# Decays of a gated linear-attention kernel taken from sums of logarithms, with a written order on every engine

## The chip, the cores and the metric

The kernel runs on one core of a Trainium2 chip. The metric is device time in microseconds (us), as the median of several executions. The before kernel's runs are 1266.61 to 1267.79 us, median 1267.73 us (3 runs). Engines are named as in the profile: PE is TensorE (matmuls), PEld its weight loads, DVE is VectorE, ACT is ScalarE, POOL is GpSimd, SP issues the DMAs.

## The reference, cut to what matters

Two blocks follow each other. The first is a recurrence over 768 time steps for each of 4 batches and 8 heads, with 48 channels a head; the second is an MLP on the 3072 tokens, with an activation h * erf(softplus(h)).

```python
f = 1.0 / (1.0 + np.exp(-f_logit))                  # (4, 8, 768, 48)
for t in range(S):
    state = f[:, :, t, :, None] * state + einsum('bhd,bhe->bhde', k[:, :, t], v[:, :, t])
    y[:, :, t] = einsum('bhd,bhde->bhe', q[:, :, t], state)
x = y.transpose(0, 2, 1, 3).reshape(3072, 384)      # heads side by side
h = x @ w_in                                        # w_in 384 x 2048, float64 in memory
sp = np.maximum(h, 0) + np.log1p(np.exp(-np.abs(h)))
out = (h * erf(sp)) @ w_out                         # w_out 2048 x 384, float64 in memory
```

The logits are drawn with mean 2 and deviation 0.5, q, k and v with mean 0 and deviation 0.1.

## The kernel before, in words

Time is cut into 24 chunks of 128 steps (6 a batch) and 8 blocks of three chunks (384 tokens). For a chunk, f, q and k are loaded with time on the partitions and turned by TensorE so that channels lie on the partitions (two heads at a time, at partitions 0 and 64). Within a chunk, output t needs the score of every earlier step s, weighted for each channel with the product of the decays between s and t. The kernel makes these without a division or a logarithm, by doubling. `scores` (line 332) computes the scores of all 8 heads and `keep` (lines 343 and 351) writes only those whose s and t first part at the current level; then `Q` is multiplied by one half's decay products on DVE (line 365), `K` by the other half's on POOL (line 369), and the products themselves are doubled on POOL (line 374). That is one set of scores at the start and one for each of seven levels, 8 sets a chunk, and set n+1 waits for the multiplications after set n. The decays come from Exp, an addition and a reciprocal (lines 313 to 315). Then `y` is summed from the kept scores `At` times v and from `Q` times the state (lines 383 and 387), copied, turned back by TensorE (`ps_x`, line 423) and copied into `xT`; the state is renewed through `ps_k`, `dS` and `S_new`.

The MLP of a block (`second_part`) has 48 matmuls into `hps` (line 255), copied by ACT to `Hg` (line 263), an activation on four groups of 128 x 1536 numbers (Exp, Ln, four Squares on ACT, four products on DVE, Tanh on ACT, one more product on DVE; lines 235 to 245), and 48 matmuls into `ops` (line 269), copied (line 278) and stored. It is a generator: `chunk` calls `pump` behind each set of scores, which issues some of the last block's matmuls there. On each engine the order is that in which a scheduler placed the program's instructions; tile pools with two buffers decide when a tile is free. The float64 weights are rounded to float32 on DVE with seven operations for each of 16 pieces of 128 x 768 (`round_piece`, lines 160 to 177); no MLP matmul stands ahead of the third chunk's end.

## Time and profile before

| what | value |
|---|---|
| median of 3 runs | 1267.73 us (1266.61 to 1267.79) |
| the profiled execution | 1266.82 us; its span 1264.8 us |
| PE busy, mean granted clock | 1045.9 us (83%), 0.889 of full speed |
| PEld, DVE, ACT, POOL busy | 693.3, 767.9, 574.3, 330.7 us |
| DMA | 37.18 MB, mean 29 GB/s |

A busy share says how long an engine had an instruction in work, not that it ran at its peak. The granted clock is 1.0 at 2.4 GHz and 0.5 at 1.2 GHz; a stretch between the two held both. A float32 matmul of the program leaves two records in the trace, a transpose one.

### The profile page before, as it was taken

To read this page: it belongs to the slowest core of one execution; us is meant where nothing else is said; L and a number is where in the kernel's file an instruction comes from. 1 tells how busy PE (TensorE), PEld (TensorE's weight loads), DVE (VectorE), ACT (ScalarE), POOL (GpSimd) and SP (SyncE) were. 2 spreads that over 40 slices of the span, in tenths; PEclk is the share of its full clock that TensorE was granted. 3 is DMA by queue.
4 is the path that set the end of the run, shared out by engine and by line. 5 is a ranking of instruction groups with operands and counts; after the bars stand their busy time and mean duration, and the time that the engine had idled before them with its cause. 6 is when DMAs were issued, how large, how long until landed. Compare 5 with 4: busy or idle time off the path is not lost.

```text
span 1264.8 us, 15677 instructions
## 1 busy us (share of the span) xinstructions
PE 1045.9 (83%) x6456; PEld 693.3 (55%) x6456; DVE 767.9 (61%) x752; ACT 574.3 (45%) x629; POOL 330.7 (26%) x369
## 2 busy tenths in 40 slices
PE   3252678898988899898978899898979899889877
PEld 2141565565655566565656566565656566556444
DVE  7979426666476816765476825864576735972262
ACT  0010114762286515771277316761387217751692
POOL 2726212213232303213232313322231312321000
PEclk9999859888888889888888889888888889888888
DMA  9530100101110110110110110110111000000000
GB/s 250 155 94 25 25 14 13 25 12 28 32 25 2 25 32 13 25 25 13 32 25 8 25 39 1 26 26 20 25 26 25 13 8 1 1 1 20 0 1 19
DMA packets 108742, 37.18 MB, mean 29 GB/s; under 512 B 100480, under 2 KB 103552, under 8 KB 108672
## 3 DMA queue, kind: packets, MB, share of 16 engines
q1 hardware_dynamic: 108672, 36.18, 13.2%
q8 instruction: 51, 0.84, 0.3%
q14 instruction: 19, 0.16, 0.0%
HBM read 31.46 MB, written 4.72 MB: 29 GB/s over the span
## 4 chain that ended last, share of the span: by engine, by line
PE 48%; DVE 21%; ACT 13%; POOL 12%; issue 5%; SPq 1%; DMA 0%; POOLq 0%; DVEq 0%; ACTq 0%
PE ops L269 15%; PE sc L332 10%; POOL K L369 8%; PE hps L255 7%; PE y L383 6%; PE y L387 5%; DVE e L241 5%; DVE F L315 5%; POOL T L374 4%; ACT x L238 3%; DVE Hg L245 2%; DVE At L343 2%; ACT z L236 2%; ACT e L235 2%; ACT L236 2%
## 5 line engine op out<-in xcount | busy, mean ns | idle before, releaser
L332 PE MATMUL sc<-Q,K 48*128 48x128 f32 (+2 forms) x3456 | 226.4, 280 | 169.7 <-POOL K L369 90.1
L332 PEld LDWEIGHTS sc<-Q,K 48*128 48x128 f32 (+2 forms) x3456 | 190.2, 184 | 271.1 <-POOL K L369 146.9
L255 PE MATMUL hps<-xT,w_in_sb 128*128 128x384 f32 x768 | 309.8, 540 | 12.0 <-ACT Hg L263 11.3
L269 PE MATMUL ops<-w_out_sb,Hg 128*128 128x384 f32 x768 | 301.9, 541 | 14.1 <-DVE Hg L245 8.8
L369 POOL TENSOR_TENSOR K<-K,T 128x256 f32<-128x256 f32 x144 | 191.9, 1333 | 354.3 <-PE sc L332 354.3
L241 DVE SCALAR_TENSOR_TENSOR e<-x,e 128x1536 f32<-128x1536 f32 x128 | 228.6, 1792 | 81.7 <-ACT x L238 81.2
L238 ACT ACTIVATE x<-z,serf_bias 128x1536 f32<-128x1536 f32 x128 | 200.4, 1572 | 83.7 <-DVE e L241 83.6
L269 PEld LDWEIGHTS ops<-w_out_sb,Hg 128*128 128x128 f32 x768 | 153.0, 210 | 114.6 <-issue 24.5
L255 PEld LDWEIGHTS hps<-xT,w_in_sb 128*128 128x128 f32 x768 | 148.2, 209 | 100.7 <-issue 19.5
L343 DVE COPY_PREDICATED At<-masks,sc 128x1024 f32<-128x1024 uint8 x144 | 186.7, 1297 | 0.1
L365 DVE TENSOR_TENSOR Q<-Q,T 128x256 f32<-128x256 f32 x144 | 80.1, 556 | 148.8 <-PE sc L332 148.7
L374 POOL TENSOR_TENSOR T<-F 128x256 f32<-128x256 f32 x24 | 34.3, 1429 | 459.0 <-DVE F L315 459.0
L351 ACT COPY At<-sc 32x256 f32<-32x256 f32 (+1 forms) x72 | 31.2, 433 | 178.1 <-PE sc L332 177.7
L263 ACT COPY Hg<-hps 128x384 f32<-128x384 f32 x128 | 58.7, 471 | 110.1 <-PE hps L255 110.0
L383 PE MATMUL y<-vt,At 128*128 128x48 f32 x384 | 84.1, 318 | 0.0
L315 DVE RECIPROCAL F<-F 128x512 f32<-128x512 f32 x24 | 80.5, 3353 | 0.8
L387 PE MATMUL y<-S_new,Q 48*128 48x48 f32 x320 | 79.8, 335 | 1.0 <-DVE Q L365 1.0
L374 POOL TENSOR_TENSOR T<-T 128x128 f32<-128x128 f32 (+1 forms) x144 | 72.1, 501 | 11.3
L383 PEld LDWEIGHTS y<-vt,At 128*128 128x128 f32 x384 | 66.2, 220 | 13.8 <-ACT At L351 0.4
L416 DVE TENSOR_TENSOR S_new<-S_new,dS 128x192 f32<-128x192 f32 x16 | 5.7, 355 | 106.4 <-PE dS L406 106.4
L278 ACT COPY osb<-ops 128x384 f32<-128x384 f32 x24 | 11.5, 479 | 127.2 <-PE ops L269 127.2
L387 PEld LDWEIGHTS y<-S_new,Q 48*128 48x128 f32 x320 | 57.8, 225 | 11.7 <-DVE Q L365 1.4
(61 smaller groups left out, 747.8 us busy)
## 6 DMA issues: line engine op xcount, KB each, us to landing
raw<-in_moe_w_in_dram SPq DMA_DIRECT2D x8, 768.0 KB, 7.5
raw<-in_moe_w_out_dram SPq DMA_DIRECT2D x8, 768.0 KB, 4.2
f_nat<-in_f_logit_dram SPq DMA_DIRECT2D x24, 192.0 KB, 3.2
q_nat<-in_q_dram SPq DMA_DIRECT2D x24, 192.0 KB, 3.9
k_nat<-in_k_dram SPq DMA_DIRECT2D x24, 192.0 KB, 3.7
vt<-in_v_dram SPq DMA_DIRECT2D x24, 192.0 KB, 2.7
out_dram<-osb SPq DMA_DIRECT2D x24, 192.0 KB, 1.9
```

Of the source, the lines that this page charges most:

```text
L238: nc.scalar.activation(out=x[:], in_=z[:], func=AF.Square, bias=serf_bias[:, i : i + 1], scale=SERF_K)
L241: nc.vector.scalar_tensor_tensor(out=e[:], in0=x[:], scalar=b, in1=e[:], op0=ALU.add, op1=ALU.mult)
L255: nc.tensor.matmul(hps[:, 0:TB], lhsT=w_in_sb[:, kt, ft * P : (ft + 1) * P], rhs=xT[:, kt, :], start=(kt == 0), stop=(kt == n_k - 1),)
L269: nc.tensor.matmul(ops[:, 0:d_model], lhsT=groups[ft // FG][:, ft % FG, tt * P : (tt + 1) * P], rhs=w_out_sb[:, ft, :], start=(ft == 0), s ...
L315: nc.vector.reciprocal(out=F[:], in_=F[:])
L332: nc.tensor.matmul(sc[s0 : s0 + size, r, a, s0 + off : s0 + off + size], lhsT=K[rows(r), a, s0 : s0 + size], rhs=Q[rows(r), a, s0 + off : ...
L343: nc.vector.copy_predicated(out=A[:].rearrange("s r a t -> s (r a) t"), mask=masks[:, level, :].unsqueeze(1).broadcast_to((P, H, P)), data ...
L365: nc.vector.tensor_tensor(out=Qv[:, :, 1, :], in0=Qv[:, :, 1, :], in1=Tv[:, :, 0:1].broadcast_to((P, n, h)), op=ALU.mult,)
L369: nc.gpsimd.tensor_tensor(out=Kv[:, :, 0, :], in0=Kv[:, :, 0, :], in1=Tv[:, :, 1:2].broadcast_to((P, n, h)), op=ALU.mult,)
L374: nc.gpsimd.tensor_tensor(out=T2[:], in0=Tv[:, :, 0], in1=Tv[:, :, 1], op=ALU.mult)
L383: nc.tensor.matmul(y_h, lhsT=A[:, r, a, :], rhs=vt[:, 2 * a + r, :], start=True, stop=(c == 0))
L387: nc.tensor.matmul(y_h, lhsT=Q[rows(r), a, :], rhs=S_old[rows(r), a, :], start=False, stop=True)
```

## The change

The decays are no longer multiplied up by levels. With c the running sum over the chunk of log(1 + exp(-logit)), q is multiplied by exp(-c) and k by exp(c), and one set of scores under a triangular mask replaces the eight. `prepare` makes the logarithms with a maximum on POOL and Exp and Ln on ACT, one call for a block's three chunks; `stage_d` sums them with one matmul by a triangular matrix, takes the two exponentials from PSUM and multiplies q on DVE and k on POOL; four DMAs bring the chunk's last row of exp(-c), which is the chunk's whole decay, onto partitions as `Tall`. `stage_t` turns q and k, `stage_s` makes the scores, masks them on DVE (`A`) and forms the new state `Mbd`. `stage_y` makes x already transposed: v and the state are the stationary operand, 32 columns each, and A or q moves, so that each matmul writes 32 partitions of `y`; no transposes or second copy follow. The rows of `w_in` are loaded in the order that this leaves.

Rounding now has an Abs on ACT, a maximum on POOL, four operations on DVE and the last addition on POOL. Hidden rows are copied from PSUM by DVE, two tiles of 384 at a time. The whole order is written by hand: `slots` yields 96 MLP matmuls for a block (the hidden matmuls of block `it` and the output matmuls of block `it - 1`), every third slot takes one step of the activation, and the 12 stages of block `it + 1` are spread over the slots. The first and the last iteration have 48 slots, and the last two have no stages. At the end the smallest whole decay is compared with `GUARD`, and where it is smaller, `general()` computes everything again by levels.

```diff
+GUARD = 4.3e-18
+LOGIT_MIN = -43.0
...
-        sc, blocks = scores(0)
-        pump(fill)
-        nc.vector.tensor_tensor(out=Q[:], in0=Q[:], in1=F[:], op=ALU.mult)
-        keep(sc, blocks, 0)
...
-        for level, h in enumerate(levels):
-            sc, blocks = scores(h)
-            pump(fill)
...
-            nc.vector.tensor_tensor(
-                out=Qv[:, :, 1, :], in0=Qv[:, :, 1, :],
-                in1=Tv[:, :, 0:1].broadcast_to((P, n, h)), op=ALU.mult,
-            )
-            nc.gpsimd.tensor_tensor(
-                out=Kv[:, :, 0, :], in0=Kv[:, :, 0, :],
-                in1=Tv[:, :, 1:2].broadcast_to((P, n, h)), op=ALU.mult,
-            )
-            T2 = work.tile([P, n], FP32, name=f"T{h}", tag=f"T{h}")
-            nc.gpsimd.tensor_tensor(out=T2[:], in0=Tv[:, :, 0], in1=Tv[:, :, 1], op=ALU.mult)
-            T = T2[:]
...
+    def y_matmuls(y, A, vt, qT, Mbd):
...
+        for i in range(2):
+            for h in range(4 * i, 4 * i + 4):
+                nc.tensor.matmul(
+                    y[M * (h % 4) : M * (h % 4 + 1), i, :],
+                    lhsT=v_heads(vt, h % 2)[:, h // 2, mains(h % 2)],
+                    rhs=A[:, h % 2, h // 2, :],
+                    start=True, stop=last, skip_group_check=True,
+                )
...
+        nc.scalar.activation(out=x.bitcast(FP32), in_=high.bitcast(FP32), func=AF.Abs)
+        nc.gpsimd.tensor_scalar(
+            out=x.bitcast(FP32), in0=x.bitcast(FP32), scalar1=TINY, scalar2=None, op0=ALU.max
+        )
         nc.vector.tensor_scalar(
+            out=x, in0=x, scalar1=0x07FFFFFF, scalar2=3,
+            op0=ALU.bitwise_and, op1=ALU.logical_shift_left,
+        )
+        nc.vector.scalar_tensor_tensor(
+            out=x, in0=high, scalar=0xC0000000, in1=x, op0=ALU.bitwise_and, op1=ALU.bitwise_or
         )
         nc.vector.tensor_scalar(
+            out=z, in0=x, scalar1=0xFF800000, scalar2=None, op0=ALU.bitwise_and
+        )
+        nc.vector.scalar_tensor_tensor(
+            out=low.bitcast(FP32), in0=low, scalar=2.0**-52, in1=z.bitcast(FP32),
+            op0=ALU.mult, op1=ALU.mult,
+        )
+        nc.gpsimd.tensor_tensor(
+            out=dst,
+            in0=low.bitcast(FP32).rearrange("p (a f) -> p a f", a=dst.shape[1]),
+            in1=x.bitcast(FP32).rearrange("p (a f) -> p a f", a=dst.shape[1]),
+            op=ALU.add,
...
+    def prepare(blk, j0, j1):
+        lt = lts[blk][:, j0:j1, :].rearrange("t j c -> t (j c)")
+        nc.gpsimd.tensor_scalar(
+            out=lt, in0=lt, scalar1=LOGIT_MIN, scalar2=None, op0=ALU.max
+        )
+        nc.scalar.activation(out=lt, in_=lt, func=AF.Exp, scale=-1.0)
+    def prepare_log(blk, j0, j1):
+        lt = lts[blk][:, j0:j1, :].rearrange("t j c -> t (j c)")
+        nc.scalar.activation(out=lt, in_=lt, func=AF.Ln, bias=1.0)
+    def stage_d(g):
+        blk, j = divmod(g, CPB)
+        ps = ps_at.tile([P, 512], FP32, name="ps_d", tag="at")
+        nc.tensor.matmul(
+            ps[:, 0:d_model], lhsT=tri[:], rhs=lts[blk][:, j, :], start=True, stop=True
+        )
+        dp = dps[g % 2]
+        dm = work1.tile([P, d_model], FP32, name="dm", tag="dm")
+        nc.scalar.activation(
+            out=dp[:, :, 0:D], in_=ps[:, 0:d_model].rearrange("t (h d) -> t h d", d=D),
+            func=AF.Exp, scale=-1.0,
+        )
+        nc.scalar.activation(out=dm[:], in_=ps[:, 0:d_model], func=AF.Exp)
+        for a in range(HP):
+            nc.sync.dma_start(
+                out=Tall[:, g, a : a + 1], in_=dp[P - 1 : P, 2 * a : 2 * a + 2, :]
+            )
+        for eng, dst, n, d in (
+            (nc.vector, qds[g % 2], qns[g % NQ], dp[:, :, 0:D]),
+            (nc.gpsimd, kds[g % 2], kns[g % NQ], dm[:].rearrange("t (h d) -> t h d", d=D)),
+        ):
+            eng.tensor_tensor(
+                out=dst[:, :, 0:D],
+                in0=n[:].rearrange("t (h d) -> t h d", d=D),
+                in1=d,
+                op=ALU.mult,
+            )
+    def stage_t(g):
+        pss = []
+        for src in (qds[g % 2], kds[g % 2]):
+            ps = ps_at.tile([P, HP, P], FP32, name="ps_t", tag="at")
+            flat = src[:].rearrange("t (a r) d -> t a (r d)", r=2)
+            for a in range(HP):
+                nc.tensor.transpose(ps[:, a, :], flat[:, a, :], ident[:])
+            pss.append(ps)
+        qTs[g] = work.tile([P, HP, P], FP32, name="qT", tag="qT")
+        kTs[g] = work1.tile([P, HP, P], FP32, name="kT", tag="kT")
+        nc.scalar.copy(out=qTs[g][:], in_=pss[0][:])
+        nc.vector.tensor_copy(out=kTs[g][:], in_=pss[1][:])
+    def stage_s(g):
+        b, c = divmod(g, NCH)
+        qT, kT = qTs[g], kTs.pop(g)
+        sc = ps_sc.tile([P, 2, HP, P], FP32, name="sc", tag="sc")
+        for a in range(HP):
+            for r in range(2):
+                nc.tensor.matmul(
+                    sc[:, r, a, :], lhsT=kT[rows(r), a, :], rhs=qT[rows(r), a, :],
+                    start=True, stop=True,
+                )
+        A = work1.tile([P, 2, HP, P], FP32, name="A", tag="A")
+        nc.vector.tensor_tensor(
+            out=A[:].rearrange("s r a t -> s (r a) t"),
+            in0=sc[:].rearrange("s r a t -> s (r a) t"),
+            in1=mask[:].unsqueeze(1).broadcast_to((P, H, P)),
+            op=ALU.mult,
+        )
+        As[g] = A
+        if c == NCH - 1:
+            return
+        dS = ps_at.tile([P, HP, D], FP32, name="dS", tag="at")
+        vt, kd = vts[g % NV], kds[g % 2]
+        for a in range(HP):
+            for r in range(2):
+                h = 2 * a + r
+                nc.tensor.matmul(
+                    dS[rows(r), a, :], lhsT=kd[:, h, 0:D], rhs=v_heads(vt, r)[:, a, :],
+                    start=True, stop=True,
+                )
...
+            nc.vector.tensor_tensor(
+                out=Sn[rows(r)], in0=dS[rows(r)], in1=old[rows(r), :, r, :], op=ALU.add
+            )
+            nc.gpsimd.tensor_tensor(
+                out=new[rows(r), :, r, :], in0=Sn[rows(r)], in1=total, op=ALU.mult
+            )
+    def stage_y(g):
+        c = g % NCH
+        blk, j = divmod(g, CPB)
+        if j == 0:
+            xTs[blk] = work.tile([P, n_k, TB], FP32, name="xT", tag="xT")
+        y = ps_at.tile([P, n_k, P], FP32, name="y", tag="at")
+        y_matmuls(y, As.pop(g), vts[g % NV], qTs.pop(g), Mbds[(g + 1) % 2] if c else None)
+        nc.scalar.copy(out=xTs[blk][:, :, j * P : (j + 1) * P], in_=y[:])
...
+        y = work1.tile([P, FG * TB], FP32, name="yl", tag="yl")
+        nc.scalar.activation(out=y[:], in_=e[:], func=AF.Ln, scale=SERF_C, bias=1.0)
+        yield
+        x = None
+        for i in range(len(SERF_AB)):
+            x_new = work.tile([P, FG * TB], FP32, name="x", tag="x")
+            squared(x_new, y, i)
+            if x is not None:
+                times(e, x, i - 1)
+            x = x_new
+            yield
+        times(e, x, len(SERF_AB) - 1)
+        yield
+        yield
         nc.scalar.activation(out=e[:], in_=e[:], func=AF.Tanh)
+        yield
         nc.vector.tensor_tensor(out=h, in0=h, in1=e[:], op=ALU.mult)
...
+                    while not gr["done"]:
+                        act_step()
...
+        if it < last:
+            return chain(
+                *(hidden(it, gi) for gi in range(n_g - 1)),
+                *(project(it - 1, [tt], whole) for tt in range(CPB)),
+                hidden(it, n_g - 1),
+            )
+        if it == last:
...
+            return chain(
+                *(hidden(it, gi) for gi in range(n_g - 1)),
+                *(project(it - 1, [tt], whole) for tt in range(CPB - 1)),
+                some(FG),
+                hidden(it, n_g - 1),
+                head,
+            )
+        return project(last, list(range(CPB)), [range(n_ft - FG), range(n_ft - FG, n_ft)])
...
+        prepare(0, 0, 1)
+        prepare_log(0, 0, 1)
+        stage_d(0)
+        prepare(0, 1, 3)
+        prepare_log(0, 1, 3)
+        stage_t(0)
+        stage_d(1)
+        stage_s(0)
+        weights_step()
+        stage_t(1)
+        stage_y(0)
+        stage_d(2)
+        stage_s(1)
+        weights_step()
+        stage_t(2)
+        stage_y(1)
+        stage_s(2)
+        load_to(3)
+        weights_step()
+        stage_y(2)
...
+            for g in range(g0, g0 + CPB):
+                last = g == n_chunks - 1
+                todo += [] if last else [(stage_d, g + 1)]
+                todo += [(stage_s, g)]
+                todo += [] if last else [(stage_t, g + 1)]
+                todo += [(stage_y, g)]
...
+            for s, _ in enumerate(slots(it)):
+                if it == 0 and s % 6 == 2:
+                    weights_step()
+                if it == 0 and s % 6 == 5:
+                    weights_step()
...
+                if at and s == at[0]:
+                    at.pop(0)
+                    f, g = todo.popleft()
+                    f(g)
+                    if f is stage_y:
+                        load_to(g + LOOK)
+                if s % 3 == 2:
+                    act_step()
+                if it + 2 < n_blocks and s == n // 2:
+                    prepare(it + 2, 0, CPB)
+                    prepare_log(it + 2, 0, CPB)
...
+        low = work.tile([P, 1], FP32, name="low", tag="low")
+        nc.vector.tensor_reduce(
+            out=low[:], in_=Tall[:].rearrange("p g a -> p (g a)"), axis=AX.X, op=ALU.min
...
+    bad = nc.values_load(flag[0:1, 0:1], min_val=0, max_val=1)
+    with tc.If(bad > 0):
+        general()
```

The places below show how the instructions stand on their engines. On PE, within a steady block of the kernel before (`sc` are sets of scores, `hps` hidden matmuls, `ops` output matmuls):

```order
L332 MATMUL sc<-Q,K 128x128 x8
L255 MATMUL hps<-xT,w_in_sb 128x384 x7
L332 MATMUL sc<-Q,K 128x128 x8
L255 MATMUL hps<-xT,w_in_sb 128x384 x2
L332 MATMUL sc<-Q,K 128x128 x8
L255 MATMUL hps<-xT,w_in_sb 128x384
L332 MATMUL sc<-Q,K 128x128 x8
L255 MATMUL hps<-xT,w_in_sb 128x384 x3
L332 MATMUL sc<-Q,K 128x128 x8
L255 MATMUL hps<-xT,w_in_sb 128x384 x5
```

Five of the eight sets of one chunk stand here between the MLP matmuls.

On PE, within a steady block now (`ps_d` is the sum of logs, `ps_t` the transposes; Hg with a number is one group's buffer):

```order
L450 MATMUL hps<-xT,w_in_sb 128x384 x7
L312 MATMUL ps_d<-lt,tri 128x384
L450 MATMUL hps<-xT,w_in_sb 128x384 x5
L476 MATMUL ops<-w_out_sb,Hg_113 128x384 x2
L356 MATMUL sc<-qT,kT 128x128 x8
L375 MATMUL dS<-vt_92,kd_102 48x48 x8
L476 MATMUL ops<-w_out_sb,Hg_113 128x384 x2
L476 MATMUL ops<-w_out_sb,Hg_114 128x384 x4
L476 MATMUL ops<-w_out_sb,Hg_115 128x384 x2
L343 MATMUL ps_t<-ident,qd_101 128x128 x4
L343 MATMUL ps_t<-ident,kd_103 128x128 x4
L476 MATMUL ops<-w_out_sb,Hg_115 128x384 x2
```

One chunk's sum, one set of scores with its `dS`, and the transposes stand about seven MLP matmuls apart.

On DVE before, while weights are rounded (`raw`, `w_x`, `w_z`, `w_e` belong to the rounding, the rest to the first chunk):

```order
L170 SCALAR_TENSOR_TENSOR w_e<-raw,w_z 128x768
L160 TENSOR_SCALAR w_x<-raw 128x768
L173 TENSOR_TENSOR w_e<-w_e,w_x 128x768
L174 TENSOR_SCALAR w_z<-raw 128x768
L164 SCALAR_TENSOR_TENSOR w_x<-raw,w_x 128x768
L177 SCALAR_TENSOR_TENSOR w_in_sb<-w_z,w_e 128x3x256
L167 TENSOR_SCALAR w_z<-w_x 128x768
L343 COPY_PREDICATED At_91<-masks,sc 128x1024
```

And now on DVE in the first MLP iteration (`w_t` and Hg_112 upward are the rounding's buffers):

```order
L273 TENSOR_SCALAR w_t<-w_t 128x768
L277 SCALAR_TENSOR_TENSOR w_t<-Hg_112,w_t 128x768
L280 TENSOR_SCALAR w_t<-w_t 128x768
L283 SCALAR_TENSOR_TENSOR Hg_112<-Hg_112,w_t 128x768
L330 TENSOR_TENSOR qd_100<-qn_95,dp_104 128x8x48
L273 TENSOR_SCALAR w_t<-w_t 128x768
L277 SCALAR_TENSOR_TENSOR w_t<-Hg_113,w_t 128x768
L280 TENSOR_SCALAR w_t<-w_t 128x768
L283 SCALAR_TENSOR_TENSOR Hg_113<-Hg_113,w_t 128x768
```

with this on POOL at the same place:

```order
L270 TENSOR_SCALAR w_t<-w_t 128x768
L287 TENSOR_TENSOR w_in_sb<-Hg_112,w_t 128x3x256
L300 TENSOR_SCALAR lt<-lt 128x768
L330 TENSOR_TENSOR kd_102<-kn_98,dm 128x8x48
L270 TENSOR_SCALAR w_t<-w_t 128x768
L287 TENSOR_TENSOR w_in_sb<-Hg_113,w_t 128x3x256
L391 TENSOR_TENSOR Mbd_107<-Sn,Tall 48x4x48 x2
L270 TENSOR_SCALAR w_t<-w_t 128x768
```

Each piece stands between a maximum and an addition on POOL, in one line with the chunks' work of that engine, and DVE's first of four operations waits for the maximum.

On ACT in a steady block now (half a block; `yl` is the activation's logarithm, `lt` the logits):

```order
L411 ACTIVATE e<-Hg_113 128x1536
L413 ACT_TABLE_LOAD
L413 ACTIVATE yl<-e 128x1536
L170 ACTIVATE x<-yl,serf_bias 128x1536 x2
L317 ACT_TABLE_LOAD
L317 ACTIVATE dp_104<-ps_d 128x8x48
L321 ACTIVATE dm<-ps_d 128x384
L170 ACTIVATE x<-yl,serf_bias 128x1536 x2
L426 ACTIVATE e<-e 128x1536
L347 COPY qT<-ps_t 128x512
L411 ACTIVATE e<-Hg_114 128x1536
L413 ACT_TABLE_LOAD
```

A block has 10 table loads: four ahead of the activation's Ln, three ahead of `stage_d`, two in `prepare`, one ahead of a Tanh.

## Rows read from the trace of the kernel before

**Rows 1.** Busy time by stretch (us): opening, two steady blocks, tail; then clock, DMA share, GB/s.

```profile
0.00:183.00 183.00, 80.15 (x597) 67.05 (x597) 132.94 (x195) 12.36 (x23) 72.16 (x61) 0.91 0.39 95
566.50:846.50 280.00, 252.99 (x1620) 166.17 (x1618) 172.43 (x154) 143.31 (x158) 75.36 (x88) 0.89 0.11 22
1160.00:1264.80 104.80, 84.37 (x237) 48.13 (x235) 35.17 (x21) 60.86 (x57) 0.01 (x1) 0.86 0.02 8
```

**Rows 2.** Groups of instructions by shape: busy us, mean ns; idle before, releasers.

```profile
L269 PE MATMUL ops<-w_out_sb,Hg 128*128 128x384 f32 x768 | 301.9, 541 | 14.1 <-DVE Hg L245 8.8 <-ACT Hg L263 5.1
...
L332 PE MATMUL sc<-Q,K 48*128 48x128 f32 x2304 | 193.3, 314 | 131.5 <-POOL K L369 57.9 <-DVE Q L365 34.7 <-ACT K L318 22.5
...
L369 POOL TENSOR_TENSOR K<-K,T 128x256 f32<-128x256 f32 x144 | 191.9, 1333 | 354.3 <-PE sc L332 354.3
```

**Rows 3.** Busy time of line 269 alone in the tail: PE, PEld, clock, DMA share, GB/s.

```profile
1246.00:1260.00 14.00, 14.00 (x44) 8.29 (x45) 1.00 0.08 28
```

**Rows 4.** Order of time on PE: start, duration (us), instruction, count, idle before.

```profile
8.65 2.08 PE L332 MATMUL sc<-Q,K 48*128 48x128 f32 x16 [0.67 <-ACT K L318]
...
361.13 0.67 PE L406 MATMUL dS<-vt,Kn 128*64 128x48 f32 x16
...
414.72 0.60 PE L298 MATMUL ps_t<-ident,q_nat 128*128 128x128 f32 x4
...
427.95 1.16 PE L332 MATMUL sc<-Q,K 48*128 48x128 f32 x16
```

**Rows 5.** Busy time, all engines (PE, PEld, DVE, ACT, POOL), then clock.

```profile
403.00:409.00 6.00, 6.00 (x23) 5.09 (x23) 0.61 (x1) 0.26 (x1) 0.00 (x0) 0.54 0.00 0
423.00:437.00 14.00, 11.35 (x76) 6.97 (x72) 13.93 (x12) 4.75 (x4) 8.95 (x11) 1.00 0.00 0
1237.00:1243.00 6.00, 5.55 (x9) 3.13 (x10) 3.82 (x3) 2.15 (x3) 0.00 (x0) 0.50 0.00 0
53.70:63.30 9.60, 0.00 (x0) 0.00 (x0) 9.60 (x15) 0.59 (x2) 9.60 (x1) 1.00 0.34 104
```

**Rows 6.** Groups by shape on ACT.

```profile
L238 ACT ACTIVATE x<-z,serf_bias 128x1536 f32<-128x1536 f32 x128 | 200.4, 1572 | 83.7 <-DVE e L241 83.6
...
L235 ACT ACTIVATE e<-Hg 128x1536 f32<-128x1536 f32 x32 | 47.5, 1484 | 1.3 <-DVE Hg L245 0.5
...
L236 ACT ACT_TABLE_LOAD x32 | 41.1, 1283 | 0.6
...
L278 ACT COPY osb<-ops 128x384 f32<-128x384 f32 x24 | 11.5, 479 | 127.2 <-PE ops L269 127.2
```

**Rows 7.** Groups by shape on DVE.

```profile
L241 DVE SCALAR_TENSOR_TENSOR e<-x,e 128x1536 f32<-128x1536 f32 x128 | 228.6, 1792 | 81.7 <-ACT x L238 81.2
...
L343 DVE COPY_PREDICATED At<-masks,sc 128x1024 f32<-128x1024 uint8 x144 | 186.7, 1297 | 0.1
...
L245 DVE TENSOR_TENSOR Hg<-Hg,e 128x1536 f32<-128x1536 f32 x32 | 55.9, 1746 | 13.6 <-ACT e L244 13.6
...
L164 DVE SCALAR_TENSOR_TENSOR w_x<-raw,w_x 128x768 uint32<-128x768 uint32 x16 | 16.0, 1001 | 0.0
L170 DVE SCALAR_TENSOR_TENSOR w_e<-raw,w_z 128x768 f32<-128x768 uint32 x16 | 15.8, 985 | 0.0
...
L167 DVE TENSOR_SCALAR w_z<-w_x 128x768 uint32<-128x768 uint32 x16 | 8.7, 546 | 0.0
L160 DVE TENSOR_SCALAR w_x<-raw 128x768 uint32<-128x768 uint32 x16 | 8.7, 551 | 5.6 <-DMA raw<-in_moe_w_in_dram 5.6
```

**Rows 8.** Groups by shape on POOL: a product of 192 numbers a partition.

```profile
L412 POOL TENSOR_TENSOR S_new<-S_new,T 128x192 f32<-128x192 f32 x16 | 8.6, 538 | 1.3
```

**Rows 9.** Order of time on POOL in the opening: two products of 256 numbers.

```profile
15.34 0.84 POOL L369 TENSOR_TENSOR K<-K,F 128x256 f32<-128x256 f32 x1 [0.97 <-PE sc L332]
...
53.68 10.17 POOL L369 TENSOR_TENSOR K<-K,T 128x256 f32<-128x256 f32 x1 [1.09 <-PE sc L332]
```

**Rows 10.** Order of time on PE in the last 30 us.

```profile
1237.45 24.12 PE L269 MATMUL ops<-w_out_sb,Hg 128*128 128x384 f32 x64 [3.77 <-DVE Hg L245]
```

## What was predicted, before the changed kernel ran

> **What bounds the kernel now.** I read the busy times by stretch first, then the groups of instructions by shape with what ended their idle time, then PE's order of time. The stretches give three parts [rows 1]: an opening of 183 us in which PE works 80 us and no MLP matmul runs, steady blocks of 140 us each (280 us for two), and a tail of 105 us. In a steady block PE is busy 126 of 140 us, so it bounds, but it is not at its peak: the mean output matmul record lasts 541 ns [rows 2], while in a stretch of output matmuls alone 44 records fill 14.00 us, 318 ns each [rows 3]. The rest is waiting and a lower clock. The scores' records alone hold 193 us, and before them PE idles 131 us, most of it until POOL's product of K or DVE's of Q is done [rows 2]. That is the chain of levels: scores, products, next scores.
>
> **The change, part by part.** I sum PE's work for a steady block, then ask which other engine comes near it, then do the opening and the tail. A matmul of the program is two records, so an MLP matmul costs 2 x 318 = 636 ns at the full clock [rows 3].
>
> *Steady block.* 96 MLP matmuls: 61.1 us. A chunk's sum of logs is one more of that size: 0.64 us. Eight transposes: four take 0.60 us [rows 4], so 1.2 us. One set of scores: 1.16 us, and `dS`, which five chunks of six have, 0.67 us [rows 4]. `y` now has 28 matmuls (16 in a batch's first chunk, 26 on average) of 32 columns by 128 moving ones, a shape that the trace does not show. Bounds from the nearest rows: scores share the array two by two and cost 1.16 / 8 = 0.145 us for 128 moving columns; `dS` costs 0.67 / 8 = 0.084 us for 48, which scaled to 128 columns, as if nothing overlapped, is 0.22 us [rows 4]; four tiles at once would be a quarter of that, 0.056 us. So `y` is 1.5 to 5.8 us a chunk; it cannot be below nothing, as PE must stream its columns. I take the scores' 0.145 us, since they have the same moving length and also go to separate parts of the array: 3.8 us. A chunk's stages are 0.64 + 1.2 + 1.16 + 0.56 + 3.8 = 7.4 us, three of them 22 us, and the block 61 + 22 = 83 us.
>
> The page "TensorEngine Tiling (Array Packing)" of the Trainium skill says, under Theoretical Speedup, that a dimension of at most 32 gives up to four times; by that `y` would be at the low end, 2.3 us less a chunk, some 41 us less over six blocks. Its Key Properties say too that a change of tiling mode drains the array, which speaks against the 12 stages strewn into a block. No run here has shown either for this shape, and the sum above goes without them.
>
> ACT in that block: 16 Squares at 1.572 us, 12 Exp, Ln or Tanh at 1.484 us, 10 table loads at 1.283 us, six exponentials, three `y` and three output copies at 0.48 us and three copies of 512 at some 0.6 us [rows 6], and Exp and Ln of 1152 numbers at three quarters of 1.484 us: 25.2 + 17.8 + 12.8 + 5.8 + 1.7 + 2.2 = 65.5 us. DVE: 16 products at 1.792 us, four at 1.746 us, eight copies of 768 and three maskings of 1024 at 1.27 ns a number (1.297 us for 1024) [rows 7], and some 2 us of small work a chunk: 28.7 + 7.0 + 7.8 + 3.9 + 6 = 53 us. POOL has about 9 us. So PE bounds, with 17 us to spare over ACT. The copies of masked scores (187 us over the kernel [rows 7]) and the products of K (192 us [rows 2]) go with their waits, and so do those of Q and the reciprocal. What is late next is the short way between stages: the transposes' second tile and the next sum take PSUM buffers that `dS` and `y` free, seven slots (4.5 us) after they were issued, while DVE may have an activation product or two (3.6 us) and a masking (1.3 us) in front. I allow 0.6 us for each of 12 stages, 7 us, between nothing and 15 us. A block is then 90 us, and six of them 540 us.
>
> Does the clock hold? PE was at 0.54 while it worked without a gap on `y` matmuls of 48 columns, and at 1.00 while scores and MLP matmuls kept it busy 11.35 of 14 us [rows 5]. The new stages take one to four us each between stretches of MLP matmuls, which is like the second row, so I take the full clock for steady blocks.
>
> *Opening.* Three chunks go through all stages before the first MLP matmul. In the opening PE runs at the 1.2 GHz pace: 16 records of scores take 2.08 us from 8.65 us on, against 1.16 us later [rows 4], although the mean clock of that stretch reads 0.91 [rows 1]. At twice the above the three chunks are 3 x (1.3 + 2.4 + 2.1) + 4.0 for three `dS` + 72 `y` matmuls at 0.29 us = 42 us. The first sum comes about when the first scores came, some 10 us in, since a maximum, Exp, a table load and Ln now stand between the logits' landing and PE. That makes 52 us to the first MLP matmul in place of 183; bounds are 42 us (`y` four at once) and 65 us (each of some 13 stages waits a microsecond more).
>
> *First iteration.* 48 slots would be 31 us and the stages 23 us on PE, but 13 of 16 pieces are rounded here. A piece has four DVE operations, 0.551 + 1.001 + 0.546 + 0.985 = 3.08 us [rows 7], and a maximum and an addition of 768 numbers on POOL. POOL's nearest row is 192 numbers in 0.538 us [rows 8], so the addition is 2.0 us; the maximum, with one input, I set between 0.5 and 2.0 us and take 1.1 us. Maximum, DVE's four and addition are one chain, and the next piece's maximum stands behind the addition on POOL, as the order shows: 13 x 6.2 = 80 us. POOL's own chunk work in between is 11 us (three products of k at 1.1 us, six of the state at 0.54 us, three maxima of logits). And the two engines do not work beside each other freely: a product of 256 numbers took 0.84 us early on and 10.17 us [rows 9] where DVE was busy throughout with rounding (the last row of [rows 5]). So of DVE's other work (activation products, about 17 us here) most comes on top: 80 + 11 + 14 = 105 us. DVE itself waits for POOL in every piece now, which gives POOL its turn, so I take 105 us. Bounds: DVE alone, 40 for rounding + 34 other = 74 us; POOL three times slower than taken, 165 us.
>
> The Trainium skill's page "SBUF — State Buffer", section "Who interferes with whom", says that a DVE instruction with two SBUF inputs and a POOL instruction that reads SBUF exclude each other for one whole instruction. By that POOL would wait at most one DVE operation, about 1 us, each time, and the first iteration would be the 105 us; the row of 10.17 us shows a wait over many operations, which is the 165 us.
>
> *Tail.* The eighth iteration has 96 slots and no stages: 63 us. In the last, 48 slots are 31 us; after eight of them PE waits for the third group's activation, whose chain is about 16 us (Exp, load, Ln, four Squares, product, Tanh, product) against 5 us of matmuls: 11 us of waiting, and then some 2.5 us lost at half clock, as before, where PE waited 3.8 us [rows 10] and then ran at 0.50 (the third row of [rows 5]): 44 us. Last copy, store, and the guard's comparison and branch: 5 us, where before it was 3 us.
>
> Sum: 52 + 105 + 540 + 63 + 44 + 5 = 809 us of span, 811 us with the 2 us that the profiled execution of before has around its span (1266.82 against 1264.8 us). That execution is 0.9 us under its median, so I predict 810 us.
>
> **The rivals.**
> 1. *ACT and DVE set the block.* For it: ACT has 65.5 of 83 us, 12.8 us of it table loads, and it waits in order for PE, DVE and POOL. Each Tanh waits 1.8 us for a product, and the sums' exponentials wait for PE. If ACT idles 35 us a block, 100 us, the six blocks cost 60 us more and the eighth iteration 10: 880 us. Against it: hidden groups are ready long before they are wanted.
> 2. *The opening hides better and `y` overlaps four ways.* First iteration at its lower bound (-30), `y` at its (-41): 740 us. Against it: [rows 9].
> 3. *Rounding starves POOL.* First iteration 165 us: 870 us. For it: the 10.17 us of [rows 9].
> 4. *Slower: the clock stays low.* The place is PE in the steady blocks. If transposes, narrow `y` matmuls and short waits keep it at 1.2 GHz as in the first row of [rows 5], the 83 us of a block become 166, and the MLP's 94 us of the tail 188: 810 + 6 x 83 + 94 = 1400 us. It decides for slower when more than (1267 - 810) / 592 = 77% of that time is at the low level. Against it: the mean of before is 0.89 with longer waits.
> 5. *The change doesn't do what it says:* the guard's branch is taken and everything runs twice, far over 2000 us. It needs a chunk decay below 4.3e-18, that is a sum of logs over 40; with logits around 2 a step gives about 0.14 and 128 steps 18. So hardly.
>
> **How the numbers follow.** My forecast, PE-bound blocks behind a serial first iteration, has 64%, with its own range of 760 to 860 us (block 83 to 98 us). Rival 1 has 12%, rival 2 13%, rival 3 8.5%, rivals 4 and 5 together 2.5%. The range reaches from 735 us, just under rival 2, to 900 us, over rivals 1 and 3. A change of 0.2% (2.5 us) is about what a measurement of this kernel can tell from none: faster 97.5%, no change 0%, slower 2.5%.
>
> **What would show it.** MLP matmuls begin near 52 us. The first iteration's 13 rounding pieces come 7 to 8 us apart, with DVE waiting for POOL. Steady blocks take 90 us, PE is busy over 90% of them at a clock of 0.97 or more, and a chunk's `y` takes 3.8 us. ACT is busy near 65 us a block. In the last iteration one wait of PE near 11 us for an activation. I am wrong if a block takes 98 us or more, if the clock sinks to 0.9, or if the first iteration is under 85 or over 130 us.

## Result: what the changed kernel takes, and its profile

The changed kernel takes 882.22 us (median of 4 runs, 881.8 to 882.34) against 1267.76 us (1266.61 to 1267.91): a ratio of 0.696, 95% interval 0.6948 to 0.6972. I had said 810 us, 735 to 900. The profiled execution has a span of 880.0 us. The 72 us between are not one error but four: +39 us in the opening, +64 in the first iteration, -38 in the six steady blocks, +6 in the tail.

The busy time by stretch of the changed kernel, to be read against [rows 1]: stretch (us), its length, PE, PEld, DVE, ACT, POOL, then granted clock, DMA share and GB/s. The stretches are the opening up to the first MLP matmul, the first iteration, two steady blocks, the eighth iteration, and the rest.

```profile
0.00:91.40 91.40, 26.47 (x271) 18.88 (x271) 17.66 (x39) 17.23 (x24) 16.79 (x20) 0.65 0.26 70
91.40:260.20 168.80, 65.30 (x385) 38.22 (x385) 67.73 (x84) 49.21 (x53) 75.50 (x41) 0.68 0.33 83
342.32:426.13 83.81, 79.81 (x471) 48.97 (x470) 52.94 (x41) 63.16 (x56) 11.16 (x8) 0.96 0.18 36
426.13:509.58 83.45, 78.71 (x463) 48.28 (x462) 54.32 (x43) 63.16 (x56) 9.56 (x8) 0.98 0.18 36
762.00:826.20 64.20, 62.48 (x193) 36.31 (x192) 43.27 (x30) 51.03 (x37) 0.00 (x0) 1.00 0.02 6
826.20:880.00 53.80, 34.79 (x98) 19.43 (x96) 19.42 (x14) 28.12 (x22) 0.00 (x0) 0.84 0.05 16
```

Read the first two lines first: in 260 us no engine is busy for even half of a stretch. Nothing is a bound there; everything waits. The blocks are the opposite: 84 us in place of 140, PE busy 79 to 80 of them near the full clock.

Where the opening waits: the order of time on PE, and on SP's queue (start, duration, instruction, count, idle before and its releaser).

```profile
69.46 1.08 PE L140 MATMUL y<-A,vt 128*32 128x128 f32 x16 [38.66 <-DVE Mbd L384]
```

```profile
11.46 45.16 SPq L255 DMA_DIRECT2D Hg<-in_moe_w_in_dram  x20
56.75 11.59 SPq L323 DMA_DIRECT2D Tall<-dp  x8
74.53 4.94 SPq L255 DMA_DIRECT2D Hg<-in_moe_w_in_dram  x5
79.56 4.85 SPq L323 DMA_DIRECT2D Tall<-dp  x4
85.68 6.41 SPq L255 DMA_DIRECT2D Hg<-in_moe_w_in_dram  x5
92.14 3.65 SPq L209 DMA_DIRECT2D lt<-in_f_logit_dram  x1
```

DVE's wait for `Tall` over the whole span (engine, line, releaser: us in total, times, longest):

```profile
DVE Mbd L384 <- DMA Tall<-dp: 47.3, 1, 47.3
```

PE stands still for 38.66 us at the first chunk's `y`, 16 matmuls that read no state. By the code they need a PSUM tile, of which there are two (tag `at`), and the first chunk's `dS` holds one until DVE has multiplied it by `Tall` into `Mbd`; `y` starts when that product ends. The transfer of `Tall`, ready early, is issued at 56.75 us, behind 20 loads of w_in that SP takes 45.16 us to issue. The logits of chunk 3 come after 30 of them, at 92.14 us. While SP is held, the DMA engines are nearly idle. The busy time from 20 to 56 us (columns as above):

```profile
20.00:56.00 36.00, 2.25 (x26) 1.59 (x24) 1.22 (x1) 1.36 (x2) 2.21 (x2) 0.55 0.16 58
```

A DMA share of 0.16 of 16 engines is the work of 2.6 of them, at 58 GB/s.

The first iteration: groups by shape from 91.4 to 260.2 us (count, busy us, mean ns; idle before, releasers).

```profile
L270 POOL TENSOR_SCALAR w_t<-w_t 128x768 f32<-128x768 f32 x14 | 29.7, 2124 | 11.5 <-ACT w_t L269 11.3
...
L287 POOL TENSOR_TENSOR w_out_sb<-Hg,w_t 128x768 f32<-128x768 f32 x8 | 20.8, 2596 | 26.1 <-DVE Hg L283 19.6 <-DMA vt<-in_v_dram 3.3 <-DMA kn<-in_k_dram 3.3
...
L287 POOL TENSOR_TENSOR w_in_sb<-Hg,w_t 128x768 f32<-128x768 f32 x6 | 11.3, 1884 | 20.7 <-DVE Hg L283 20.7
...
L300 POOL TENSOR_SCALAR lt<-lt 128x384 f32<-128x384 f32 (+2 forms) x3 | 7.9, 2637 | 24.7 <-DMA lt<-in_f_logit_dram 24.7
L170 ACT ACTIVATE x<-yl,serf_bias 128x1536 f32<-128x1536 f32 x5 | 7.9, 1575 | 34.3 <-POOL w_out_sb L287 32.4 <-POOL w_in_sb L287 1.9
...
L273 DVE TENSOR_SCALAR w_t<-w_t 128x768 uint32<-128x768 uint32 x14 | 7.8, 559 | 64.0 <-POOL w_t L270 64.0
...
L312 PE MATMUL ps_d<-lt,tri 128*128 128x384 f32 x8 | 5.8, 817 | 53.7 <-ACT lt L307 53.7
```

POOL's maximum of 768 numbers lasts 2.12 us, where I had taken 1.1. DVE waits for it 64 us, ACT's Square waits 34 us for POOL's addition, PE 54 us for logits, POOL 25 us for their load. At least three causes are in this, and the trace alone does not say what each is worth. That is what the experiments had to tell.

A steady block: order of time on PE, one chunk's `y`, and the one long wait of the block.

```profile
368.94 0.43 PE L140 MATMUL y<-A,vt 128*32 128x128 f32 x8
369.19 0.40 PE L147 MATMUL y<-qT,Mbd 128*32 128x128 f32 x8
369.40 0.40 PE L140 MATMUL y<-A,vt 128*32 128x128 f32 x8
369.62 0.40 PE L147 MATMUL y<-qT,Mbd 128*32 128x128 f32 x8
369.84 0.62 PE L155 MATMUL y<-A,vt 128*32 128x128 f32 x16
370.28 0.40 PE L162 MATMUL y<-qT,Mbd 128*32 128x128 f32 x8
370.61 4.78 PE L450 MATMUL hps<-xT,w_in_sb 128*128 128x384 f32 x14
...
393.66 6.10 PE L476 MATMUL ops<-w_out_sb,Hg 128*128 128x384 f32 x10 [4.00 <-DVE Hg L428]
```

The 28 matmuls of `y` fill 370.61 - 368.94 = 1.67 us, not 3.8.

### The profile page after: what moved, and what is told of

Its sections match the earlier page's. It is cut to its first block, busy times and chain, and to the rows that moved or that the text cites. A ratio compares the mean times of both kernels' runs of the same rounds, so it can differ in the third digit from the quotient of the medians.

```text
span 880.0 us, 9394 instructions
## 1 busy us (share of the span) xinstructions
PE 663.2 (75%) x3729; PEld 403.6 (46%) x3729; DVE 474.7 (54%) x419; ACT 528.8 (60%) x465; POOL 152.5 (17%) x107
## 4 chain that ended last, share of the span: by engine, by line
PE 53%; issue 14%; DVE 11%; ACT 8%; POOL 6%; DMA 4%; SPq 3%; POOLq 0%; ACTq 0%; DVEq 0%
PE ops L476 24%; PE hps L450 21%; DVE e L175 5%; DVE Hg L428 2%; POOL w_t L270 2%; PE sc L356 2%; DMA Hg<-in_moe_w_in_dram 2%; POOL w_out_sb L287 2%; ACT e L426 1%; PE ps_d L312 1%; SPq L216 1%; PE ps_t L343 1%; PE y L140 1%; SPq L255 1%; ACT x L170 1%
## 5 line engine op out<-in xcount | busy, mean ns | idle before, releaser
L476 PE MATMUL ops<-w_out_sb,Hg 128*128 128x384 f32 x768 | 273.6, 509 | 40.8 <-DVE Hg L428 40.2
L450 PE MATMUL hps<-xT,w_in_sb 128*128 128x384 f32 x768 | 270.6, 506 | 10.9 <-DVE Hg L457 10.3
L170 ACT ACTIVATE x<-yl,serf_bias 128x1536 f32<-128x1536 f32 x128 | 198.9, 1574 | 59.0 <-POOL w_out_sb L287 38.0
L330 POOL TENSOR_TENSOR kd<-kn,dm 128x384 f32<-128x384 f32 x24 | 29.1, 1213 | 367.6 <-ACT dm L321 240.7
L457 DVE COPY Hg<-hps 128x768 f32<-128x768 f32 x64 | 61.1, 954 | 53.0 <-PE hps L450 51.8
L428 DVE TENSOR_TENSOR Hg<-Hg,e 128x1536 f32<-128x1536 f32 x32 | 62.7, 1959 | 21.7 <-ACT e L426 21.6
L426 ACT ACTIVATE e<-e 128x1536 f32<-128x1536 f32 x32 | 47.5, 1484 | 37.5 <-DVE e L175 37.5
L411 ACT ACTIVATE e<-Hg 128x1536 f32<-128x1536 f32 x32 | 47.2, 1475 | 7.6 <-DVE Hg L457 7.6
L413 ACT ACTIVATE yl<-e 128x1536 f32<-128x1536 f32 x32 | 47.5, 1483 | 0.4
L312 PEld LDWEIGHTS ps_d<-lt,tri 128*128 128x128 f32 x48 | 10.1, 226 | 73.9 <-ACT lt L307 60.3
L270 POOL TENSOR_SCALAR w_t<-w_t 128x768 f32<-128x768 f32 x16 | 34.0, 2124 | 20.7 <-ACT w_t L269 20.4
```

The source lines that it names most:

```text
L170: nc.scalar.activation(out=dst[:], in_=y[:], func=AF.Square, bias=serf_bias[:, i : i + 1], scale=SERF_K)
L270: nc.gpsimd.tensor_scalar(out=x.bitcast(FP32), in0=x.bitcast(FP32), scalar1=TINY, scalar2=None, op0=ALU.max)
L312: nc.tensor.matmul(ps[:, 0:d_model], lhsT=tri[:], rhs=lts[blk][:, j, :], start=True, stop=True)
L330: eng.tensor_tensor(out=dst[:, :, 0:D], in0=n[:].rearrange("t (h d) -> t h d", d=D), in1=d, op=ALU.mult,)
L411: nc.scalar.activation(out=e[:], in_=h, func=AF.Exp)
L413: nc.scalar.activation(out=y[:], in_=e[:], func=AF.Ln, scale=SERF_C, bias=1.0)
```

## Experiments

Each run was timed beside the kernel before, which took 1265.7 to 1266.5 us there. "Opening" ends at the first MLP matmul; "first iteration" ends where the next one's first MLP matmul starts; "rest" is what remains of the span. All three are read from PE's order of time in each run's trace; in the two runs without rounding the end of the first iteration lies within one entry of that order and is worked out from the count of its matmuls.

| run | time, us | ratio to before (95%) | opening | first iteration | rest |
|---|---|---|---|---|---|
| changed kernel | 882.22 | 0.696 (0.6948 to 0.6972) | 91.4 | 168.8 | 619.8 |
| bands | 826.25 | 0.652 (0.6507 to 0.6533) | 60.0 | 145.9 | 618.6 |
| tall_on_act | 873.06 | 0.6891 (0.6879 to 0.6902) | 60.3 | 191.7 | 619.0 |
| no_round | 817.27 | 0.6444 (0.6431 to 0.6457) | 87.2 | 111 | 618 |
| bands_no_round | 752.43 | 0.5942 (0.5928 to 0.5956) | 51.0 | 81 | 619 |
| own_tag | 818.71 | 0.6465 (0.6453 to 0.6477) | 58.2 | 139.2 | 620.5 |
| all_dve | 798.94 | 0.6313 (0.63 to 0.6326) | 58.7 | 118.4 | 619.7 |
| own_tag_all_dve | 793.27 | 0.6263 (0.6251 to 0.6275) | 60.7 | 112.3 | 619.5 |
| cadence | 815.28 | 0.6439 (0.6427 to 0.645) | 60.6 | 145.9 | 608.2 |
| early_f | 779.66 | 0.6162 (0.6151 to 0.6173) | 61.3 | 96.9 | 619.3 |
| tall_on_act_2 | 786.96 | 0.6213 (0.6203 to 0.6223) | 44.0 | 121.5 | 619.9 |
| best | 754.96 | 0.5962 (0.5952 to 0.5972) | 44.9 | 101.3 | 606.8 |

The rest is the same to 2.5 us wherever the activation steps are not moved, so each edit to the loads or to rounding can be read from the first two columns alone.

### bands: other shape of the w_in loads

```diff
-            for a in range(HP):
-                full = pairs[a, 0:M, :]
-                src = bass.AP(
-                    tensor=full.tensor, offset=full.offset,
-                    ap=[[(2 * D - M) * full.ap[0][0], 2], *(list(x) for x in full.ap)],
-                )
-                parts.append((a // 2, slice(2 * M * (a % 2), 2 * M * (a % 2 + 1)), src))
+            for a in range(2):
+                for r in range(2):
+                    at = (2 * D - M) * r
+                    parts.append((
+                        0, slice(2 * M * a + M * r, 2 * M * a + M * (r + 1)),
+                        pairs[a::2, at : at + M, :].rearrange("x e f -> e x f"),
+                    ))
```

> Edit: the four loads of a w_in piece that begin with a dimension of 2 now begin with one of 32 (32 rows, two pairs of heads each); the same bytes, the same 5 loads a piece, the same places in memory; each goes to 32 partitions in place of 64. Theory A (a load that begins with a dimension of 2 runs on few DMA engines, and Tall waits in SP's queue behind 20 of them): SP issues the 20 loads in 12 to 22 us in place of 45.16, the first MLP matmul comes at 55 to 65 us in place of 91.4, and the first iteration, whose logits stand in the same queue, loses 10 to 35 of its 169 us: total 810 to 850 us. Theory B (loads to a part of the partitions are slow as such): 45 us or more for the 20 loads, total 880 us or more. Theory C (queue as in A, but the first iteration is set by rounding alone): opening as in A, first iteration still 160 to 170 us, total 845 to 855 us.

SP's queue (columns as above), and the busy time from 13 to 29 us:

```profile
12.16 16.79 SPq L258 DMA_DIRECT2D Hg<-in_moe_w_in_dram  x20
29.08 7.86 SPq L326 DMA_DIRECT2D Tall<-dp  x8
```

```profile
13.00:29.00 16.00, 6.60 (x42) 4.44 (x42) 1.84 (x3) 6.96 (x9) 4.11 (x3) 1.00 0.69 163
```

The same bytes in the same number of loads take 16.79 in place of 45.16 us, at a DMA share of 0.69 in place of 0.16, and with fewer partitions a load. Theory A holds in the queue, the opening, the first iteration and the total; B falls; C falls too, as the first iteration lost 23 us. The Trainium skill has the rule that I should have weighed: "DMA: Bandwidth & Descriptors", section "Why a DMA increments its semaphore by 16 and not by 1", says that a transfer is dealt to at most 16 engines, to the largest number up to 16 that divides the outermost dimension (over 1) of both sides, and to the lowest-numbered ones. By that the loads that begin with 2 all ran on the same two engines. The shares of 0.16 and 0.69 agree with it; which engines moved the bytes these rows do not show.

### tall_on_act: Tall past the queue

```diff
-            nc.sync.dma_start(
+            (nc.scalar if g < LOOK else nc.sync).dma_start(
                 out=Tall[:, g, a : a + 1], in_=dp[P - 1 : P, 2 * a : 2 * a + 2, :]
```

> Edit: the loads of Tall for the first three chunks are issued by ACT instead of SP; the w_in loads stay as they are. Theory A (the first y matmuls wait only because Tall stands behind 20 loads in SP's queue): the first MLP matmul at 55 to 65 us, total 845 to 860 us, unless the rounding of the late pieces gives part back. Rival (Tall's own transfer, 128 numbers of 4 bytes on the same few DMA engines, is what takes the time: 8 of them took 11.59 us to issue): the first MLP matmul later than 75 us, total over 865 us.

The opening ends at 60.3 us, as theory A has it, with the slow loads left alone: the queue, not `Tall`'s own transfer, made the wait. But 23 of the 31 us were given back, and the total of 873 us is outside theory A's 845 to 860. SP's queue shows why:

```profile
11.98 71.02 SPq L255 DMA_DIRECT2D Hg<-in_moe_w_in_dram  x30
83.04 2.48 SPq L209 DMA_DIRECT2D lt<-in_f_logit_dram  x1
```

The logits of chunk 3 still come after 30 loads of w_in, at 83.04 us in place of 92.14: 9 us sooner, while PE is 31 us sooner. POOL now waits 29.6 us for them in one go, everything behind them runs some 8 to 10 us earlier, and the total falls by 9 us. PE is merely early for the next late transfer.

### no_round and bands_no_round: rounding taken out

```diff
-        nc.scalar.activation(out=x.bitcast(FP32), in_=high.bitcast(FP32), func=AF.Abs)
-        nc.gpsimd.tensor_scalar(
...
-            op=ALU.add,
-        )
+        nc.vector.tensor_scalar(
+            out=dst,
+            in0=high.bitcast(FP32).rearrange("p (a f) -> p a f", a=dst.shape[1]),
+            scalar1=0.02, scalar2=None, op0=ALU.mult,
+        )
```

> Edit: rounding is left out; a piece of weights is one DVE operation (high word times 0.02), with no Abs on ACT and no maximum and addition on POOL; all loads stay. It leaves out the rounding of w_in and w_out. Theory R (the chain ACT, POOL, DVE, POOL of rounding sets the first iteration, with POOL's maximum at 2.12 us): the opening stays near 88 to 91 us and the first iteration falls from 169 to 85 to 110 us: total 795 to 825 us. Theory Q (late loads in SP's queue set it): the first iteration stays at 145 us or more, total 855 us or more.

> Edit: both the loads of 32 rows and no rounding (it leaves out the rounding of the weights). If the two causes are apart, the first MLP matmul comes at 52 to 60 us and the first iteration takes 75 to 95 us: total 755 to 785 us. If one hides behind the other, the gain is less than the sum of the two gains by as much as they share; if the first iteration stays over 120 us, neither is what sets it.

Without rounding the first iteration is 111 us, 1 us above theory R's range, and the total of 817 us is inside it; so R holds for about 58 of the 169 us, and Q falls. 111 us is still well over the 31 us of its MLP matmuls and the 3 x (0.8 + 1.2 + 1.2 + 0.6 + 1.7) = 16.5 us of its stages, so something else, the loads by the next run, holds part of it too. With both edits 81 us are left, and opening and total (51 and 752 us) are a little under what I had expected. The two gains, 56 and 65 us, come to 130 together, 9 more than their sum. I had expected less than the sum where one cause hides behind the other; it is the other way round, since what still holds the stretch keeps part of a gain back until it is gone as well.

### own_tag, all_dve, own_tag_all_dve: which part of rounding

The edit of own_tag, that of all_dve, and in own_tag_all_dve both:

```diff
-        t = work.tile([P, 2, PIECE], U32, name="w_t", tag="x")
+        t = work.tile([P, 2, PIECE], U32, name="w_t", tag="w_t")
```

```diff
-        nc.gpsimd.tensor_scalar(
+        nc.vector.tensor_scalar(
             out=x.bitcast(FP32), in0=x.bitcast(FP32), scalar1=TINY, scalar2=None, op0=ALU.max
...
-        nc.gpsimd.tensor_tensor(
+        nc.vector.tensor_tensor(
             out=dst,
```

> Edit, on top of the loads of 32 rows (826.25 us, first iteration 145.9 us, a piece each 11 us): the tile w_t of rounding gets buffers of its own, where it shared two with the x of the activation. Theory S (ACT's Square, which writes x, waits in order until POOL's addition has freed the buffer, and the next piece's Abs stands behind that Square, so that a piece is one ring ACT, POOL, DVE, POOL, ACT): a piece falls to 6 to 8 us, the first iteration to 95 to 125 us, total 775 to 806 us, and ACT's wait for POOL's addition, 32.4 us in that stretch, is gone. Rival D (POOL's maximum and addition, 2.1 and 1.9 to 3.3 us, and DVE's four operations one after the other set the pace whatever the buffers): first iteration 138 us or more, total 818 us or more.

> Edit, on top of the loads of 32 rows: the maximum and the addition of rounding run on DVE in place of POOL, buffers shared as before. Theory S (the ring sets the pace): the ring is shorter by POOL's 2.1 + 1.9 to 3.3 us and longer by some 1.5 us on DVE, so 13 pieces gain 30 to 50 us: first iteration 95 to 116 us, total 776 to 796 us. Rival (POOL was slow only because DVE kept it out, and DVE's time counts instead): DVE would have 13 x 4.6 + 34 = 94 us of work in a row with waits between, first iteration 125 us or more, total 805 us or more.

> Edit, on top of the loads of 32 rows: both of these, buffers of its own for w_t and maximum and addition on DVE. Theory S: with the ring open, DVE's sum of work bounds the first iteration, 13 x 4.6 + 34 = 94 us: 88 to 102 us, total 767 to 783 us. If it takes no less than the better of the two single edits, they pay for the same wait.

Theory S, my first reading of ACT's wait of 32 us, fell: with buffers of its own that wait was gone, but the iteration lost 7 us only, and both numbers, 139 and 819 us, are in rival D's range. The waits of own_tag from 60 to 200 us (engine, line, releaser: us in total, times, longest) show what had come in its place:

```profile
ACT lt L306 <- POOL lt L303: 36.1, 3, 16.6
ACT x L170 <- DVE e L175: 25.7, 3, 13.6
...
DVE w_t L276 <- POOL w_t L273: 48.5, 12, 9.7
```

ACT now waited for the logits' maximum on POOL and for DVE's products, and DVE, as before, for POOL's maximum of weights. Taking both operations from POOL brought 27.5 us, the largest gain in this stretch from an edit that keeps the work, and a little less than the 30 to 50 that theory S gave; 118 and 799 us lie between it and its rival, far nearer to S. With both edits the iteration was 112 us, above the 88 to 102 that I expected when DVE's work bounds it: DVE was busy 89 of these 112 us. What was left stood in own_tag_all_dve's waits:

```profile
ACT lt L306 <- POOL lt L303: 20.8, 3, 13.9
...
POOL lt L303 <- DMA lt<-in_f_logit_dram: 19.9, 2, 16.7
```

### early_f: logits ahead of the weights

```diff
+        for g in range(LOOK, 2 * CPB):
+            load_f(g)
         for _ in range(4):
             next_piece()
...
-                if loaded[0] < 2 * CPB:
-                    load_f(loaded[0])
```

> Edit, on top of own_tag_all_dve (793.27 us; opening 60.7 us, first iteration 112.3 us): the logits of chunks 3 to 5 are loaded ahead of the first four w_in pieces, not behind five and six of them. Theory F (the first iteration still waits for logits that stand in SP's queue; PE waits 28.9 us for lt, POOL 19.9 us for their load): these waits fall under 15 us and the first iteration to 95 to 106 us, the opening is 0 to 3 us longer: total 776 to 788 us. Rival (DVE's work, 94 us by my sum, bounds it now, so another wait comes in their place): first iteration 108 us or more, total 789 us or more.

The first iteration falls by 15 us to 96.9, the opening grows by 0.6. POOL's wait for the logits' load up to 200 us, and PE's wait for the logits over the whole span:

```profile
POOL lt L303 <- DMA lt<-in_f_logit_dram: 1.9, 2, 1.4
```

```profile
PE ps_d L315 <- ACT lt L310: 12.7, 3, 7.4
```

Theory F holds.

### tall_on_act_2

> Edit, on top of own_tag_all_dve: the loads of Tall of the first three chunks are issued by ACT. Theory O (with w_in's loads short, y's wait of 13.4 us for Tall goes and what the opening gains is kept): first MLP matmul at 46 to 53 us, total 778 to 786 us. Rival G (the opening's gain is given back, as it was when only Tall was moved: 31 us sooner at the first MLP matmul, 23 us longer in the first iteration, since the weights' pieces are rounded no sooner): total 789 to 795 us.

The edit is that of tall_on_act, made on own_tag_all_dve. The opening gains 16.7 us and ends at 44.0; the first iteration gives 9.2 of them back. Neither theory has the whole: the logits were late again, POOL waited 31.0 us for them.

### cadence: activation steps sooner in a block

```diff
-                if s % 3 == 2:
+                if s % 5 in (1, 4) if 0 < it < n_blocks and s < 48 else s % 3 == 2:
                     act_step()
```

> Edit, on top of the loads of 32 rows: in the first half of the iterations 1 to 7 a step of an activation is taken in two of five slots in place of one of three. Theory W (PE waits 4 us in each block at slot 48 because the last group's activation has come too few steps): the waits go, the six blocks cost 3 to 4.5 us less each, total 798 to 810 us. Rival (ACT's or DVE's own time is short there, so the wait only moves): within 5 us of 826 us.

PE's waits over the whole span, in bands and then in cadence:

```profile
PE ops L479 <- DVE Hg L431: 40.2, 8, 11.9
...
PE hps L453 <- DVE Hg L460: 9.9, 2, 8.8
PE ps_t L346 <- DVE Sn L391: 8.5, 1, 8.5
```

```profile
PE hps L453 <- DVE Hg L460: 22.2, 8, 8.8
PE ps_t L346 <- DVE Sn L391: 16.7, 4, 8.5
...
PE ops L479 <- DVE Hg L431: 6.1, 1, 6.1
```

Of 34 us that the wait for the activation lost, 20 came back as waits behind the same DVE, whose products now stand ahead of a PSUM copy or a state. The rest of the program fell by 10 us and the total by 11, to 815 us, between the two theories.

### best: all together

> Edit: loads of 32 rows, w_t in buffers of its own, maximum and addition on DVE, early logits, Tall of the first three chunks on ACT, and the cadence of activation steps, all together. If the gains add up: 793 - 10 (cadence) - 10 (logits) - 5 (Tall) = 768 us, 755 to 780 us. If the first iteration is bounded by DVE's 94 us, the logits and Tall bring nothing: 780 to 786 us.

754.96 us, 127 us under the changed kernel and 511 under the kernel before beside it. The gains add up, to the lower end of the range of 755 to 780; that logits and `Tall` bring nothing is refuted. Its first iteration, by the busy time:

```profile
44.90:146.20 101.30, 60.28 (x385) 36.27 (x385) 90.89 (x110) 50.53 (x54) 13.02 (x11) 0.83 0.53 134
```

DVE is busy 91 of 101 us: here the stretch has a bound at last, and it is close to the 94 us of DVE's work that I had summed.

## Why the prediction came out where it did

**Opening, 52 said, 91.4 measured.** The step that failed is one that I did not take. I priced the stages at half clock and allowed a microsecond of waiting for each, up to 65 us; I did not follow SP's queue. `Tall` is a DMA that the change adds, it stands behind 20 loads, and the change had also cut each load of 768 KB into five with a new first dimension. In the trace of before eight whole pieces are issued in 17.93 us from 12.85 us on:

```profile
12.85 17.93 SPq L148 DMA_DIRECT2D raw<-in_moe_w_in_dram  x8
```

I took it for granted that pieces of another shape go as fast. With the loads reshaped the opening is 60.0 us, and with `Tall` on another queue as well 44.0, inside my bounds of 42 to 65. That this end fits is luck, though. The opening of best by the busy time:

```profile
0.00:44.90 44.90, 25.31 (x270) 17.69 (x270) 22.20 (x46) 17.45 (x24) 10.90 (x19) 1.00 0.67 151
```

PE works 25 us in it, not the 42 that I summed, most of the difference being `y`, about 7 us there where I had 21; the first sum comes at 7.6 us, not 10; and some 12 us are waits, for which my sum had nothing.

**First iteration, 105 said, 169 measured.** I had the chain of rounding right and its links partly mis-sized: POOL's addition, 1.9 to 2.6 us, is near my 2.0, but its maximum takes 2.12 us, not 1.1, and with that my own sum is 118 us. Undisturbed, two pieces start 7.2 to 8.6 us apart (maxima at 238.02, 245.22 and 253.86 us), as I had said; over the whole stretch it is (253.86 - 93.04) / 13 = 12.4 us. In own_tag, with short loads and separate buffers, the first and the last of the eleven maxima behind the late logits are

```profile
99.35 2.12 POOL L273 TENSOR_SCALAR w_t<-w_t 128x768 f32<-128x768 f32 x1
...
191.10 2.12 POOL L273 TENSOR_SCALAR w_t<-w_t 128x768 f32<-128x768 f32 x1
```

which is 9.2 us a piece, the chunks' work included, or 119 us for 13, as much as my sum with the maximum at its true size. What I had put at nothing is the rest: 23 us for the w_in loads' shape (bands) and 7 for the shared buffers (own_tag). Of the 20 us then left, own_tag's first three pieces have 15: they take 43 us (56.28 to 99.35), with the logits of chunks 3 to 5 between them. POOL waits 5.8 us for the load of logits there, and early_f gains 15 us on another kernel, so the share of the logits is an estimate. In the order of the runs the edits take off 23 us (loads), 27.5 (POOL's two operations), 6 (buffers) and 15 (logits), down to 97 us, but that is no check of the 105, which had POOL's two operations in it. The order matters, since the causes overlap. Of the term itself I had left out that ACT, POOL and DVE each stand in order, so that a late logit holds a rounding step and a rounding step holds a stage.

**Steady blocks, 90 said, 83.6 measured.** The shape of the sum held: PE bounds, ACT takes 63.2 us (65.5 said), DVE 53 to 54 (53 said), the clock is 0.96 to 0.98. `y` was mis-sized: I took the scores' 0.145 us a matmul, it is 1.67 / 28 = 0.060, next to my lower end of 0.056. That is 2.1 us a chunk, 6.4 us a block, as much as the whole difference. "TensorEngine Tiling (Array Packing)" of the Trainium skill, section "Theoretical Speedup", has up to four times for a dimension of 32; these rows agree, and I should have given that end more weight. Two smaller errors cancel. Stalls were 4.0 to 4.7 us in one place, an activation that is late for the output matmuls, and not 0.6 us at each of 12 stages, 7 us in all. And PE's work without the error in `y` is 2 to 3 us more than my sum, most of it behind that stall: the ten records that follow it fill 6.0 us at a granted clock of 0.56, near the lower of the two levels, where ten take 3.2 us at the full clock.

**Tail, 112 said, 118 measured.** The eighth iteration is 64.2 us (63 said); PE's wait in the last is 11.88 us (11 said); the last iteration and the end are 3 and 2 us longer than said.

**The rivals.** ACT and DVE do not set the block: ACT idles 20 us of it. The clock stays up. The guard's branch is not taken: the end is 7 us. Rival 2 was right in `y` (38 of its 41 us came) and wrong in the first iteration, which it had 30 us shorter. Rival 3 gave 165 us for the first iteration, near the measured number, but its mechanism, POOL kept out over many DVE operations as in [rows 9], does not show: POOL's longest addition is 3.29 us where the undisturbed one is 1.84. The sum 810 + 39 + 64 - 38 + 6 = 881 closes on 882; that errors of both signs met is why the range held.

## What to carry to other kernels

When a change recuts a load or adds a small one, read the queue as a list of everything ahead of it, and for each load look at the first dimension of both sides before taking over a rate from a load of another shape. Where several engines in a row each work in order, take the chain's period from its longest undisturbed stretch and then look for the transfer that each link waits for. Removing one wait of such a ring (own_tag) shows little until the others go too.

## What the hardware showed that I had not expected

- While four loads in five had a first dimension of 2, 0.16 of the DMA engines were busy at 58 GB/s; with the same bytes led by 32 rows, 0.69 at 163 GB/s. The fifth load begins with 4 in both kernels.
- POOL's maximum of 768 numbers against a constant, 2.12 us, is slower than its addition of two such tiles, 1.84 us. The same maximum on DVE, in all_dve, takes 0.56 us (median of 16).
- POOL and DVE hold each other up, for one instruction at a time. Orders of time of the changed kernel, POOL and then DVE:

```profile
184.23 3.28 POOL L287 TENSOR_TENSOR w_out_sb<-Hg,w_t 128x768 f32<-128x768 f32 x1 [3.26 <-DMA vt<-in_v_dram]
...
208.97 1.84 POOL L287 TENSOR_TENSOR w_out_sb<-Hg,w_t 128x768 f32<-128x768 f32 x1 [3.26 <-DVE Hg L283]
```

```profile
184.07 1.75 DVE L175 SCALAR_TENSOR_TENSOR e<-x,e 128x1536 f32<-128x1536 f32 x1
...
209.41 3.02 DVE L175 SCALAR_TENSOR_TENSOR e<-x,e 128x1536 f32<-128x1536 f32 x1
```

At 184 us DVE's product begins first and lasts its 1.75 us, and POOL's addition ends 1.7 us after it, at 187.51. At 209 us POOL begins first, and DVE's product ends 1.6 us after the addition's end at 210.81. In both pairs the one that comes second waits for one instruction and then takes its own time. "SBUF — State Buffer" of the Trainium skill, section "Who interferes with whom", describes such an exclusive hold; these rows agree with it.
